# Putting together weight chunks 29 to 40 in SBUF instead of PSUM

## The chip, the core and the metric

One core of a Trainium2 chip runs the whole program once. The metric is the device time of that run in microseconds (us); lower is better. The core has five engines that matter here: PE (TensorE, matrix products), DVE (VectorE) and ACT (ScalarE) for elementwise work, POOL (GpSimd), and SP, which only starts transfers. PSUM is the memory that PE writes its products to, in eight banks; SBUF is the large on-chip memory.

## The reference

Attention with a mask comes first, then two dense blocks on the 1536 tokens that it gives.

```python
x = attention(q, k, v, proj)                  # 2 x 8 heads, 768 tokens, 64 wide -> (1536, 512)
xn = x / sqrt(mean(x * x) + 1e-6) * rms_g
g = xn @ w_gate                               # (512, 1536)
val = xn @ w_val
x = (g * sigmoid(g) * val) @ w_out            # (1536, 512)
h = maximum(x @ w_in, 0)                      # (512, 2048)
out = (h * h) @ w_out2                        # (2048, 512)
```

Inputs and output are float32. PE gets each float32 matrix as a rounded "high" part and the "low" remainder, and computes three products (high by high, high by low, low by high).

## The kernel before

**Weights.** They arrive as 104 chunks of 128 rows by 512 numbers, each as 64-bit floating-point numbers (512 KB). The list `mats` (line 926 on) gives their order: for each of the 12 steps f of the first dense block a gate, a value and an output chunk, all this twice (a first pass for token blocks 0 and 1, a second for 2 and 3), then 32 chunks for the second dense block. A chunk goes through these steps (`plan_weights`):

- SP loads it into `wraw` (3 buffers, line 943).
- ACT takes the absolute value of the upper 32 bits into a work tile (`w_abs`, line 956).
- DVE turns this into a float32 in place with four instructions: line 962 (clamp) and line 967 (two shifts), which read only the work tile, and lines 972 and 976, which join it with the sign and the low bits from `wraw`.
- ACT (line 305), or in some cases POOL (line 309), rounds it to the high part `wih` or `woh`; DVE subtracts for the low part `wil` or `wol` (line 314). Then the work tile is free.

**Where the work tile lies.** `apart(m)` (line 936) decides: inside `mats[WP[0]:WP[1]]` it is a tile `mo`, a PSUM bank; otherwise it is a tile `wv` in SBUF, of which there are four.

```python
t = wst[m]["v"] = mo() if apart(m) else junk()
```

The same `mo` banks take PE's products (lines 1012, 1108, 1119): three banks at first, five after the first half of attention, eight after all of it.

**Dense work around it.** For a step f and a token block PE makes the gate and the value product: 12 instructions of line 1012 each, an "in" block. ACT takes tanh of the gate (1023), DVE multiplies (1027, 1032), ACT or POOL rounds to `yh`, DVE subtracts to `yl`. After every two steps PE makes four output products a token block (1108, an "out" block of 6 instructions) that DVE adds to `acc` (1133). At the end of a pass the sums are split into high and low parts too (`xTF`, `xTG`). The token blocks' inputs are `xTA`, `xTB` in the first pass and `xTD`, `xTE` in the second.

**What sets the order.** A planner (`Plan.run`) walks all instructions with a table of assumed costs, always taking the one that can start first, and so fixes the order of each engine; each engine then runs its list in that order. For a chunk in SBUF the planner assumes 0.335 instead of 0.602 for lines 962 and 967, lets POOL or DVE do the rounding as well as ACT, and keeps DVE and POOL apart in time:

```python
D=0.335 if n < 2 and not far else 0.602, port=not far,
```

Of the kernel before, what the change touches and what calls it, by code (L numbers as in the profile page):

```python
# [54 lines left out]
WR = 3  # L55
WV = 4

WP = (6, 40)
MB = (3, 4)
G = 2  # L60

# [181 lines left out]
def tile_hash_attention_moe(  # L243
# [692 lines left out]
    def apart(m):  # L936

        return m in mats[WP[0]:WP[1]]

# [395 lines left out]
```

## Time and profile before

| what | us |
|---|---|
| median of three runs | 837.7 |
| lowest and highest | 836.83, 839.05 |
| the profiled execution itself | 836.23 |
| its span, first to last instruction | 834.4 |
| PE busy in the span | 793.3 |
| DVE busy in the span | 705.2 |
| ACT busy in the span | 452.4 |
| POOL busy in the span | 223.8 |

A busy time says how long an engine worked, not whether the end waited for it: that is read from the chain that ended last and from the idle time of each engine in a stretch. The start of a row is the time since the first instruction. Matmuls are pipelined: a row of 0.33 us is followed by the next 0.17 us later, so the distance between starts is the price of one.

### The profile page before, as it was taken

What the parts mean: (1) busy time and instruction counts of PE and PEld (TensorE: products, weight loads), DVE (VectorE), ACT (ScalarE), POOL (GpSimd) and SP (SyncE); (2) the same over time, 40 slices, a digit from 0 to 9 for tenths busy, and PEclk for the clock granted to TensorE, in tenths of its full rate; (3) what the DMA queues carried; (4) which work ended last, traced back from release to release, by engine and by line L of the source; (5) the groups of instructions that cost most, each with busy time, mean ns of one, the idle gap of its engine ahead of it and who ended that gap; (6) DMA issues with size and microseconds to landing.
All of it is one profiled execution on the core that took longest, in us unless ns stands there. A gap on an engine that the chain in (4) does not pass through costs nothing.

```text
span 834.4 us, 14958 instructions
## 1 busy us (share of the span) xinstructions
PE 793.3 (95%) x5633; PEld 721.5 (86%) x5633; DVE 705.2 (85%) x1393; ACT 452.4 (54%) x922; POOL 223.8 (27%) x195
## 2 busy tenths in 40 slices
PE   8998887899998998989999999999999999999998
PEld 4787776788887898988889999999899898998996
DVE  6996889798788789989999999999687787877764
ACT  5788887767888677433455344446542242332320
POOL 7578955556567444000000000000000000000000
PEclk8999999999999899999999999999999999999999
DMA  7577784589979797223324334333231120211003
GB/s 224 156 136 145 148 192 127 120 178 177 238 153 187 156 212 171 77 76 101 127 101 148 105 126 129 126 125 95 83 101 45 58 76 30 97 51 51 26 1 151
DMA packets 127728, 100.69 MB, mean 121 GB/s; under 512 B 106548, under 2 KB 108596, under 8 KB 127656
## 3 DMA queue, kind: packets, MB, share of 16 engines
q1 hardware_dynamic: 124160, 90.92, 43.2%
q10 hardware_dynamic: 3496, 8.81, 4.0%
q8 instruction: 44, 0.72, 0.4%
q14 instruction: 28, 0.23, 0.1%
HBM read 67.12 MB, written 3.15 MB: 84 GB/s over the span
## 4 chain that ended last, share of the span: by engine, by line
PE 71%; DVE 20%; ACT 3%; DMA 3%; issue 2%; POOL 1%; ACTq 0%; SPq 0%; DVEq 0%; POOLq 0%
PE mo L1012 33%; PE mo L1119 16%; PE mo L1108 8%; PE S L549 5%; PE O L623 4%; PE S L428 3%; DVE Pa L560 2%; DMA Ta<-hla 2%; DVE mo L962 2%; DVE acc L1133 1%; DVE mo L967 1%; DVE mo L972 1%; DVE Px L560 1%; DVE Tx L314 1%; DVE mo L976 1%
## 5 line engine op out<-in xcount | busy, mean ns | idle before, releaser
L314 POOL TENSOR_TENSOR hla<-Pa,hla 128x768 f16<-128x768 f32 x66 | 110.0, 1669 | 75.1 <-ACT hla L305 67.8
L1133 DVE TENSOR_TENSOR acc<-acc,mo 128x512 f32<-128x512 f32 (+1 forms) x164 | 101.0, 617 | 25.0 <-PE mo L1119 22.9
L549 PE MATMUL S<-k,q 76*128 76x384 f32 (+1 forms) x384 | 92.2, 365 | 12.3 <-DVE Pa L560 7.1
L1038 ACT ACTIVATE mt<-mo 128x384 f32<-128x384 f32 x64 | 31.3, 489 | 100.8 <-PE mo L1012 97.5
L549 PEld LDWEIGHTS S<-k,q 76*128 76x128 f32 (+1 forms) x384 | 65.8, 194 | 18.8 <-DVE Pa L560 9.3
L1119 PE MATMUL mo<-woh,yl 128*128 128x512 f32 x192 | 75.3, 392 | 0.0
L1119 PE MATMUL mo<-wol,yh 128*128 128x512 f32 x192 | 75.2, 392 | 0.0
L1119 PE MATMUL mo<-woh,yh 128*128 128x512 f32 x192 | 74.7, 389 | 0.0
L560 DVE TENSOR_SCALAR_CACHE_REDUCE Pa<-S 128x768 f32<-128x768 f32 x66 | 62.7, 950 | 10.9 <-PE S L549 10.2
L309 POOL TENSOR_SCALAR yh<-mu 128x384 fp32r<-128x384 f32 x20 | 10.8, 541 | 221.6 <-PE mo L1119 88.0
L1042 DVE TENSOR_TENSOR mu<-mt 128x384 f32<-128x384 f32 x64 | 35.4, 553 | 36.0 <-ACT mt L1038 35.9
L1108 PE MATMUL mo<-yh,woh 128*128 128x384 f32 x192 | 64.8, 337 | 0.7 <-ACT woh L305 0.7
L314 DVE TENSOR_TENSOR yl<-mu,yh 128x384 fp32r<-128x384 f32 x112 | 61.8, 559 | 4.1 <-POOL yh L309 2.6
L578 ACT ACTIVATE Pa<-Pa,b 128x768 f32<-128x768 f32 x66 | 62.0, 943 | 5.2 <-DVE sum L631 1.3
L1108 PE MATMUL mo<-yh,wol 128*128 128x384 f32 x192 | 64.5, 336 | 0.1
L1108 PE MATMUL mo<-yl,woh 128*128 128x384 f32 x192 | 64.2, 335 | 0.0
L309 POOL TENSOR_SCALAR wih<-wv 128x512 fp32r<-128x512 f32 x12 | 7.5, 627 | 209.1 <-ACT mt L1038 109.7
L956 ACT ACTIVATE wv<-wraw 128x512 f32<-128x512 f32 x70 | 46.6, 671 | 26.3 <-DMA wraw<-in_w 24.9
L305 ACT CAST hla<-Pa 128x768 f16<-128x768 f32 x66 | 55.0, 835 | 5.8 <-DVE wv L972 1.5
L1012 PE MATMUL mo<-xTAh,wih 128*128 128x384 f32 x160 | 55.2, 345 | 2.3 <-DVE acc L1133 2.3
L1012 PE MATMUL mo<-xTBh,wih 128*128 128x384 f32 x160 | 55.2, 345 | 2.1 <-DVE mu L1032 2.1
L1012 PE MATMUL mo<-xTAh,wil 128*128 128x384 f32 x160 | 54.5, 340 | 0.3 <-DVE wil L314 0.3
(167 smaller groups left out, 2343.8 us busy)
## 6 DMA issues: line engine op xcount, KB each, us to landing
wraw<-in_w SPq DMA_DIRECT2D x104, 512.0 KB
rk<-in_k ACTq DMA_DIRECT2D x14, 384.0 KB
vr<-in_v SPq DMA_DIRECT2D x8, 384.0 KB
out<-acc SPq DMA_DIRECT2D x12, 256.0 KB
q<-q SPq DMA_DIRECT2D x15, 192.0 KB
rq<-in_q ACTq DMA_DIRECT2D x14, 192.0 KB
Ta<-hla SPq DMA_TRANSPOSE x66
rk<-in_k SPq DMA_DIRECT2D x2, 384.0 KB
```

Of the source, the lines that this page charges most:

```text
L305: nc.scalar.copy(out_, in_)
L314: engine[eng].tensor_tensor(out=out_, in0=in0, in1=in1, op=ALU.subtract)
L549: nc.tensor.matmul(sp[:, hf, 0:TB], d[a][0:kr, t * 128:(t + 1) * 128], d[b2][0:kr, hf * TB:(hf + 1) * TB], start=(n == 0), stop=(n == 1),)
L560: nc.vector.tensor_scalar(out=e["P"].rearrange("p (a b) -> p a b", a=2), in0=e["sp"][:, :, 0:TB], scalar1=-1e9 / SCALE, scalar2=None, op0= ...
L578: nc.scalar.activation(e["P"], e["P"], AF.Exp, bias=e["b"], scale=SCALE)
L623: nc.tensor.matmul(d["O"][:, t, 0:w], T[:, a, :], b2[:, c, :], start=(c == 0 and n == 0), stop=(c == QT - 1 and n == 2),)
L956: nc.scalar.activation(t, f32(wst[m]["hi"]), AF.Abs)
L1012: nc.tensor.matmul(ps, a[:, c * 128:(c + 1) * 128], b2[:, c, :], start=(c == 0 and n == 0), stop=(c == 3 and n == 2),)
L1042: nc.vector.tensor_tensor(out=us["u"], in0=st["t"], in1=st["t"], op=ALU.mult)
L1108: nc.tensor.matmul(po, a[:, dc * 128:(dc + 1) * 128], b2, start=(j == 0 and n == 0), stop=(j == len(fs) - 1 and n == 2),)
L1119: nc.tensor.matmul(po, a[:, tt * 128:(tt + 1) * 128], b2, start=(j == 0 and n == 0), stop=(j == len(fs) - 1 and n == 2),)
L1133: nc.vector.tensor_tensor(out=ac, in0=ac, in1=st["p"], op=ALU.add)
```

## The change

One number in the range of chunks that use PSUM.

```diff
-WP = (6, 40)
+WP = (6, 28)
```

The 7th to 28th chunk of `mats` stay in PSUM. The 29th to 40th, twelve chunks, get a `wv` tile in SBUF as all later ones have: the value and output chunks of step 9, all of steps 10 and 11 of the first pass, all of step 0 and the gate of step 1 of the second. Since the planner sees other costs, all engines but SP get another order from there on; the instructions before are the same ones in the same order. PE's list differs over some 412 rows. Its first difference: after the gate of step 9 on `xTA` it now takes the gate on `xTB`, where it took the value on `xTA`.

DVE, where the lists part. First before: `mo` in a weight row is a work tile in PSUM, `wv` one in SBUF.

```order
L962 TENSOR_SCALAR mo<-mo 128x512
L1133 TENSOR_TENSOR acc_2614<-acc_2614,mo 128x384
L967 TENSOR_SCALAR mo<-mo 128x512
L972 SCALAR_TENSOR_TENSOR mo<-wraw,mo 128x512 x2
L1032 SCALAR_TENSOR_TENSOR mu<-mu,mo 128x384
L976 SCALAR_TENSOR_TENSOR mo<-wraw,mo 128x512
L1133 TENSOR_TENSOR acc_2614<-acc_2614,mo 128x384
L962 TENSOR_SCALAR mo<-mo 128x512
L314 TENSOR_TENSOR yl<-mu,yh 128x384 x2
L1133 TENSOR_TENSOR acc_2614<-acc_2614,mo 128x384
```

The same place now, still on DVE.

```order
L962 TENSOR_SCALAR wv<-wv 128x512
L1133 TENSOR_TENSOR acc_2614<-acc_2614,mo 128x384
L967 TENSOR_SCALAR wv<-wv 128x512
L972 SCALAR_TENSOR_TENSOR mo<-wraw,mo 128x512
L972 SCALAR_TENSOR_TENSOR wv<-wraw,wv 128x512
L976 SCALAR_TENSOR_TENSOR mo<-wraw,mo 128x512
L1032 SCALAR_TENSOR_TENSOR mu<-mu,mo 128x384
L1133 TENSOR_TENSOR acc_2614<-acc_2614,mo 128x384
L976 SCALAR_TENSOR_TENSOR wv<-wraw,wv 128x512
L1133 TENSOR_TENSOR acc_2614<-acc_2614,mo 128x384
L314 TENSOR_TENSOR wol<-mo,woh 128x512
L314 TENSOR_TENSOR yl<-mu,yh 128x384 x2
```

The second chunk's clamp (the second line 962) has moved behind the sums into `acc_2614`, and the output chunk (`wol`) is finished earlier.

DVE again, at the end of the first pass, where the last `xTGl` are made. Before:

```order
L314 TENSOR_TENSOR xTGl<-acc_2614,xTGh 128x384 x2
L1027 SCALAR_TENSOR_TENSOR mu<-mt,mo 128x384
L314 TENSOR_TENSOR wil<-wv,wih 128x512
L962 TENSOR_SCALAR wv<-wv 128x512
L972 SCALAR_TENSOR_TENSOR mo<-wraw,mo 128x512
L1027 SCALAR_TENSOR_TENSOR mu<-mt,mo 128x384
L967 TENSOR_SCALAR wv<-wv 128x512
L962 TENSOR_SCALAR wv<-wv 128x512
L972 SCALAR_TENSOR_TENSOR wv<-wraw,wv 128x512
L1032 SCALAR_TENSOR_TENSOR mu<-mu,mo 128x384
```

And now:

```order
L314 TENSOR_TENSOR xTGl<-acc_2614,xTGh 128x384 x2
L1027 SCALAR_TENSOR_TENSOR mu<-mt,mo 128x384
L972 SCALAR_TENSOR_TENSOR wv<-wraw,wv 128x512
L967 TENSOR_SCALAR wv<-wv 128x512
L976 SCALAR_TENSOR_TENSOR wv<-wraw,wv 128x512
L972 SCALAR_TENSOR_TENSOR wv<-wraw,wv 128x512
L1027 SCALAR_TENSOR_TENSOR mu<-mt,mo 128x384
L314 TENSOR_TENSOR wil<-wv,wih 128x512
L976 SCALAR_TENSOR_TENSOR wv<-wraw,wv 128x512
L962 TENSOR_SCALAR wv<-wv 128x512
L967 TENSOR_SCALAR wv<-wv 128x512
L314 TENSOR_TENSOR wil<-wv,wih 128x512
```

The first `wil` here (value of step 1, second pass) stands four weight instructions later behind the `xTGl`; the second (gate of step 2) follows it much sooner.

POOL, from the end of attention on, as a piece of the difference.

```order
-L309 TENSOR_SCALAR yh<-mu 128x384 x4
-L309 TENSOR_SCALAR wih<-wv 128x512 x3
-L309 TENSOR_SCALAR yh<-mu 128x384 x2
+L309 TENSOR_SCALAR yh<-mu 128x384
+L309 TENSOR_SCALAR wih<-wv 128x512
+L309 TENSOR_SCALAR yh<-mu 128x384
+L309 TENSOR_SCALAR xTGh<-acc_2614 128x384
+L309 TENSOR_SCALAR yh<-mu 128x384
+L309 TENSOR_SCALAR woh<-wv 128x512
+L309 TENSOR_SCALAR yh<-mu 128x384
```

POOL takes over the rounding of one weight chunk and of one piece of `xTG` in the changed stretch.

## Rows read from the trace of the kernel before

**Rows 1.** The page's part 4: the chain that ended last, by engine.

```profile
PE 71%; DVE 20%; ACT 3%; DMA 3%; issue 2%; POOL 1%; ACTq 0%; SPq 0%; DVEq 0%; POOLq 0%
```

**Rows 2.** Busy by stretch: PE, PEld, DVE, ACT, POOL, clock, DMA share, GB/s.

```profile
355.00:430.00 75.00, 68.76 (x370) 66.55 (x368) 71.07 (x132) 28.37 (x55) 1.54 (x3) 0.95 0.28 92
...
434.00:596.00 162.00, 161.99 (x923) 160.18 (x922) 157.76 (x315) 74.62 (x141) 9.85 (x16) 1.00 0.38 124
596.00:834.40 238.40, 234.62 (x1178) 212.11 (x1176) 171.30 (x312) 77.72 (x152) 5.59 (x10) 1.00 0.18 60
```

**Rows 3.** PE in time: start, length, instruction, idle before it and its releaser.

```profile
360.39 0.34 PE L1108 MATMUL mo<-yh,wol 128*128 128x384 f32 x1
363.03 0.45 PE L1012 MATMUL mo<-xTAh,wih 128*128 128x384 f32 x1 [2.30 <-DVE acc L1133]
...
376.50 0.41 PE L1108 MATMUL mo<-yh,woh 128*128 128x384 f32 x1 [0.68 <-ACT woh L305]
...
397.40 0.44 PE L1012 MATMUL mo<-xTBh,wih 128*128 128x384 f32 x1 [2.13 <-DVE mu L1032]
...
409.71 0.44 PE L1012 MATMUL mo<-xTDh,wil 128*128 128x384 f32 x1 [0.75 <-DVE wil L314]
...
430.20 0.44 PE L1012 MATMUL mo<-xTDh,wih 128*128 128x384 f32 x1 [0.30 <-ACT wih L305]
431.68 0.44 PE L1012 MATMUL mo<-xTDh,wil 128*128 128x384 f32 x1 [0.86 <-DVE wil L314]
```

**Rows 4.** PE again, two pairs of neighbours after the first long gap.

```profile
365.06 0.53 PE L1012 MATMUL mo<-xTAh,wih 128*128 128x384 f32 x1
365.38 0.53 PE L1012 MATMUL mo<-xTAl,wih 128*128 128x384 f32 x1
...
369.07 0.33 PE L1012 MATMUL mo<-xTBl,wih 128*128 128x384 f32 x1
369.24 0.33 PE L1012 MATMUL mo<-xTBh,wil 128*128 128x384 f32 x1
```

**Rows 5.** Groups of DVE instructions by line, 355 to 432 us: count, busy, mean ns, idle before.

```profile
L967 DVE TENSOR_SCALAR mo<-mo 128x512 uint32<-128x512 uint32 x13 | 9.0, 691 | 0.1
...
L962 DVE TENSOR_SCALAR mo<-mo 128x512 f32<-128x512 f32 x12 | 8.3, 692 | 0.0
L1027 DVE SCALAR_TENSOR_TENSOR mu<-mt,mo 128x384 f32<-128x384 f32 x11 | 6.0, 545 | 3.0 <-ACT mt L1023 3.0
...
L967 DVE TENSOR_SCALAR wv<-wv 128x512 uint32<-128x512 uint32 x3 | 1.3, 418 | 0.0
```

**Rows 6.** DVE in time: neighbours whose starts give the price of each kind.

```profile
356.51 0.69 DVE L962 TENSOR_SCALAR mo<-mo 128x512 f32<-128x512 f32 x1
...
380.32 0.69 DVE L967 TENSOR_SCALAR mo<-mo 128x512 uint32<-128x512 uint32 x1
380.92 0.54 DVE L1133 TENSOR_TENSOR acc<-acc,mo 128x384 f32<-128x384 f32 x1
381.38 0.68 DVE L314 TENSOR_TENSOR wil<-mo,wih 128x512 fp32r<-128x512 f32 x1
...
427.41 0.41 DVE L962 TENSOR_SCALAR wv<-wv 128x512 f32<-128x512 f32 x1
427.75 0.68 DVE L972 SCALAR_TENSOR_TENSOR wv<-wraw,wv 128x512 uint32<-128x512 uint32 x1
...
430.95 0.68 DVE L314 TENSOR_TENSOR wil<-wv,wih 128x512 fp32r<-128x512 f32 x1
```

**Rows 7.** POOL and DVE in time, where a POOL copy overlaps a DVE instruction.

```profile
420.70 0.51 POOL L309 TENSOR_SCALAR yh<-mu 128x384 fp32r<-128x384 f32 x1 [28.45 <-PE mo L1108]
...
420.83 0.93 DVE L976 SCALAR_TENSOR_TENSOR wv<-wraw,wv 128x512 uint32<-128x512 uint32 x1
```

**Rows 8.** DVE in time: its two longest idle pieces between 434 and 500 us.

```profile
444.84 0.43 DVE L962 TENSOR_SCALAR wv<-wv 128x512 f32<-128x512 f32 x1 [0.72 <-ACT wv L956]
467.58 0.56 DVE L1027 SCALAR_TENSOR_TENSOR mu<-mt,mo 128x384 f32<-128x384 f32 x1 [1.44 <-ACT mt L1023]
```

## The prediction

> **What bounds the kernel now.** I read the chain that ended last first: PE has 71% of it, DVE 20% [rows 1]. A mean over stages hides where the 20% lie, so the busy times by stretch come next [rows 2]. From 434 to 596 us PE works 161.99 of 162 us, and from 596 to the end 234.62 of 238.4, where what is missing is the last store. There PE is the bound, and whatever starts it earlier ends the program earlier. From 355 to 430 us it works 68.76 of 75 us while DVE works 71.07 and the mean clock is 0.95: there DVE is the bound. This is the stretch of the twelve chunks. So the third view is PE in time [rows 3]: the reader should see six of PE's seven waits (the seventh is 0.2), each for a product of DVE or for an ACT step that stands right behind one: a sum that frees a bank (2.30), a high part of an output weight (0.68), a `mu` (2.13), low parts of weights (0.75 and 0.86), a high part (0.30). The fourth view shows what the long gaps cost afterwards [rows 4]: 1.2 us after the gap of 2.30 neighbouring matmuls start 0.32 us apart instead of 0.17, the lower of the two clock levels (1.2 instead of 2.4 GHz), for some eleven instructions; eleven times 0.147 is 1.6 us.
>
> **How much PE can win at most.** From the last matmul before the first gap (start 360.39, next slot 360.56) to the matmul that starts at 431.68 [rows 3] PE makes 20 in-blocks of 12 and 16 out-blocks of 6 instructions, then two more. At 0.1733 us each (0.17 between neighbours at the higher clock [rows 4]) that is 20 x 2.08 + 16 x 1.04 + 0.35 = 58.6 us. It takes 71.1 us. So 12.5 us are gaps and low clock, more than the 7 us of idle time that the rows print, because a row's modelled end covers some of each gap. 12.5 us is the ceiling.
>
> **What the change takes from DVE.** Twelve chunks, two instructions each (lines 962 and 967), go from PSUM to SBUF. In this same stretch they last 692 and 691 ns on `mo`, 418 on `wv` [rows 5]; what DVE pays is the distance between starts: 0.60 on `mo` (380.32 to 380.92), 0.34 on `wv` (427.41 to 427.75) [rows 6]. The saving is 24 x 0.26 = 6.2 us. Lines 972 and 976 and the subtract also change memory, but they last the same on `mo` and on `wv` (the `mo` and `wv` subtracts both 0.68 [rows 6]); nothing there. ACT's steps have both forms too and ACT is busy 28.4 of 75 us [rows 2], so a few hundredths for each are hidden; were they not, 24 of them at 0.04 would be 1 us. SP's list is the same, and a load's buffer is freed by line 976, which comes earlier.
>
> **How this reaches PE.** I follow the DVE list from 356.51, where the lists part, to the low part of the second pass's step-2 gate, for which PE waits until 431.68 [rows 3, 6]. Before, 132 instructions lead there: 68 weight steps at 0.60, 59 of 384 columns at 0.465 (0.46 between 380.92 and 381.38), 5 fast ones at 0.34; in all 69.9 us. The real way is 430.95 + 0.60 - 356.51 = 75.0. The 5.1 us between are DVE's own waits, 3.0 of them for tanh [rows 5], and small dependences. In the new list 126 instructions lead there: 42 at 0.60, 56 at 0.465, 28 at 0.34, in all 60.8 us, 9.1 less. 6.0 of this are 23 faster instructions, the rest six others now put behind it (three at 0.60, three at 0.465: 3.2). If all waits stay, this low part is ready at 431.55 - 9.1 = 422.4; gapless, PE would ask for it at 431.68 - 12.5 = 419.2. The 3.0 us of waits for tanh should go: they stand at a place where PE had just lost 2.3 us to a bank and 1.6 to the clock, and two more free banks remove that first wait. (That PE has no bank is what the releaser of 363.03 says: a sum, line 1133, frees one. The two work tiles of the step-9 value and the step-10 gate held two of eight there.)
>
> In return DVE, now faster, reaches sums before PE has finished them. Placing both lists side by side at these prices, the first five weights are in time by 0.5 to 3 us, and the step-1 value of the second pass is late: PE would ask at 414.7, and DVE has it at 415.3 without any wait, near 416.8 with 1.5 us of waits. Its four weight steps now stand behind all of `xTG`. So PE stops there for about 2 us. The six instructions that were put behind must then be done before the next output blocks: 3.2 us, of which I leave half on the path, 1.5. That half also stands for a low clock after the 2 us gap (1.6 by rows 4, if it comes). Sum: 12.5 - 2.0 - 1.5 = **9.0 us**. Against the profiled execution (836.2, span 834.4) that gives 827.2; the median lies 1.5 above that execution, so **828.7**.
>
> **A price that only appears in SBUF.** At 420.83 line 976 on a `wv` lasts 0.93 instead of 0.68 us, while POOL copies from 420.70 to 421.21 [rows 7]: 0.25 lost. In the changed stretch POOL makes some six copies; DVE's list now offers more that they can hit. Six at 0.25 to 0.35 are 1.5 to 2.1 us at worst, and nothing if each falls beside an instruction that reads PSUM, or while PE is ahead. I take nothing beyond the reserve above and keep 2.1 for the range.
>
> The Trainium skill (SBUF — State Buffer, Who interferes with whom) speaks against the change here: a DVE instruction that uses both SBUF port pairs, or reads two SBUF inputs while GpSimd reads, blocks fully until the other is done. Its price for one copy is then the copy's whole length, an estimate of 0.5 to 0.6, and the gain would be 9.0 - 6 x 0.55 = 5.7 us. The row agrees in direction but shows half the price.
>
> **The rivals.**
>
> *Only DVE's own saving arrives.* If DVE meets as many waits as now (for sums, tanh, high parts of ACT), it ends the stretch 6.2 us earlier, not 9. For it: the sums of a block of four cannot be taken faster than PE makes them, 1.04 us apart. Against it: 3.0 of the waits have a cause that goes. 837.7 - 6.2 = 831.5; with the port's 2.1, 833.6.
>
> *The gain is given back after 434 us.* DVE works 157.76 of 162 us there [rows 2]; its largest pauses are 0.72 and 1.44 [rows 8]. If PE gets ahead by 2 us more than DVE, it may run dry there. Each dry spell like those of now costs 2.3 and 1.5 for the clock; two give 837.7 - 9 + 7.6 = 836.3, no change. Against it: DVE is early by about as much as PE (9.1 and 9), the order there is nearly the same, and DVE was on time from the same kind of start (PE waiting for it at 431.68).
>
> *Slower: the four `wv` tiles.* A chunk's first ACT step must wait until the subtract of the fourth chunk before it is done, and ACT, in order, keeps tanh and casts waiting behind it; PE then has no bank and no weight. With PSUM there were eight. If this holds PE by 1.3 us a chunk, 12 x 1.3 = 15.6 eat the 12.5: 837.7 - 12.5 + 15.6 = 840.8; it decides from 1.04 us a chunk on. Against it: from 434 us on all chunks go through these four tiles at the same pace, and PE has no gap [rows 2].
>
> That the change does not do what it says is hardly possible: the same two lines show both prices within this stretch [rows 5].
>
> **How the numbers follow.** The forecast (8 to 12.5 us won) gets 0.60, only DVE's saving (4 to 8 won) 0.22, given back 0.10, slower 0.06; 0.02 is left for more than the ceiling. Faster or slower by over 0.3% is 2.5 us, about what a measurement of this kernel can tell from no change. Faster: 0.60 + 0.22 + 0.02 = 0.84; same 0.10; slower 0.06. The range takes in the first two cases with the port's price: 837.7 - 12.5 = 825.2 to 833.6.
>
> **What would show it right or wrong.** Lines 962 and 967 run twelve times less on `mo` and twelve times more on `wv`, there at about 0.42 us. The gap of 2.30 at 360.7 and the low clock behind it are gone. PE's idle time up to its last wait falls from 7 to about 2 us, its largest piece at a low part of a weight some 14 us before PE becomes gapless. From there to the end the trace is the old one, earlier. I am wrong if PE has new gaps after 425 us (rival two), if ACT waits for a subtract before line 956 (rival three), or if the lines on `wv` last clearly longer than 0.42 on average (the port).

## The result, and the profile after

| | before | after |
|---|---|---|
| median of five runs, us | 837.7 | 832.02 |
| lowest and highest, us | 836.14, 839.82 | 827.13, 832.87 |
| profiled execution, us | 836.23 | 829.23 |
| its span, us | 834.4 | 827.4 |
| PE, DVE busy, us | 793.3, 705.2 | 790.9, 697.8 |

The ratio is 0.9914, with a 95% interval of 0.9889 to 0.9938: by the ratio 7.2 us are won, by the medians 5.7. The same kernel timed again, beside 23 runs of before, gave 0.9928 (0.9911 to 0.9944), 6.0 us. The forecast was 9.0.

First the chain that ended last, by engine, of the kernel after.

```profile
PE 58%; DVE 30%; DMA 4%; issue 3%; ACT 2%; POOL 1%; ACTq 0%; SPq 0%; DVEq 0%; POOLq 0%
```

DVE's share is larger than before (20% [rows 1]), though DVE works 7.4 us less and the kernel is shorter. The chain names one releaser at each step; where PE and DVE keep pace, either may be named. The share says where to look and isn't a price.

Busy time by stretch (PE, PEld, DVE, ACT, POOL, clock, DMA share, GB/s). The stretches are times since the first instruction, so from 425 us on each holds work that came up to 8 us later before:

```profile
355.00:425.00 70.00, 67.82 (x377) 66.48 (x376) 67.91 (x138) 29.70 (x55) 3.86 (x5) 0.98 0.36 113
...
434.00:596.00 162.00, 161.16 (x909) 158.16 (x908) 149.95 (x301) 74.38 (x140) 8.05 (x13) 1.00 0.36 117
596.00:827.40 231.40, 227.66 (x1144) 206.00 (x1142) 170.14 (x310) 74.44 (x147) 5.55 (x10) 1.00 0.19 62
```

Against [rows 2]: PE lacked 6.2 us of work in the 75 of the old first stretch and lacks 2.2 of 70 now; the stretch from 434 to 596, all but gapless before, now lacks 0.8. From the first instruction of line 1119 on nothing differs but where it starts: the rest takes 251.0 us before (834.4 less 583.4) and 250.9 now (827.4 less 576.5).

PE in time (start, length, instruction, idle before and its releaser): the place of the old gap of 2.30, the first of the instructions that waited, and the old last wait.

```profile
360.00 0.33 PE L1012 MATMUL mo<-xTAh,wih 128*128 128x384 f32 x1
...
414.64 0.34 PE L1012 MATMUL mo<-xTEh,wil 128*128 128x384 f32 x1
416.65 0.44 PE L1012 MATMUL mo<-xTDh,wih 128*128 128x384 f32 x1 [1.67 <-ACT wih L305]
...
417.67 0.44 PE L1012 MATMUL mo<-xTDh,wil 128*128 128x384 f32 x1 [0.40 <-DVE wil L314]
...
419.12 0.52 PE L1012 MATMUL mo<-xTDh,wih 128*128 128x384 f32 x1
419.44 0.52 PE L1012 MATMUL mo<-xTDl,wih 128*128 128x384 f32 x1
...
422.31 0.34 PE L1012 MATMUL mo<-xTEl,wih 128*128 128x384 f32 x1
...
423.55 0.33 PE L1012 MATMUL mo<-xTDh,wil 128*128 128x384 f32 x1
...
548.88 0.34 PE L1108 MATMUL mo<-yl,woh 128*128 128x384 f32 x1
550.04 0.44 PE L1108 MATMUL mo<-yh,wol 128*128 128x384 f32 x1 [0.82 <-DVE wol L314]
```

The bank gap at the start (2.30 [rows 3]) is gone, and of the seven waits of before none is left at its place. Three are new: two for the step-1 value weight of the second pass (1.67 and 0.40), with a low clock behind them (neighbours 0.32 apart; the granted clock from 419.1 to 422.3 us is 0.50, the level of 1.2 GHz), and some 132 us later 0.82 for an output weight. The step-2 gate's third instruction starts at 423.55 instead of 431.68 [rows 3], 8.1 us earlier.

DVE's lines from 355 to 425 us (count, busy, mean ns, idle before):

```profile
L962 DVE TENSOR_SCALAR wv<-wv 128x512 f32<-128x512 f32 x15 | 6.5, 436 | 0.3 <-ACT wv L956 0.3
L967 DVE TENSOR_SCALAR wv<-wv 128x512 uint32<-128x512 uint32 x15 | 6.2, 418 | 0.1
...
L1027 DVE SCALAR_TENSOR_TENSOR mu<-mt,mo 128x384 f32<-128x384 f32 x11 | 6.0, 545 | 0.0
```

The two lines now run on `wv` at 436 and 418 ns instead of 692 and 691 on `mo`, and the 3.0 us for which line 1027 waited for tanh [rows 5] are 0.0.

### The profile page after: what moved, and what is told of

The parts are those of the page before. It is cut to its first block, busy times and chain, and to the rows that moved or that the text cites. A ratio compares the mean times of both kernels' runs of the same rounds, so it can differ in the third digit from the quotient of the medians.

```text
span 827.4 us, 14953 instructions
## 1 busy us (share of the span) xinstructions
PE 790.9 (96%) x5633; PEld 720.2 (87%) x5633; DVE 697.8 (84%) x1393; ACT 454.1 (55%) x923; POOL 224.2 (27%) x194
## 4 chain that ended last, share of the span: by engine, by line
PE 58%; DVE 30%; DMA 4%; issue 3%; ACT 2%; POOL 1%; ACTq 0%; SPq 0%; DVEq 0%; POOLq 0%
PE mo L1012 23%; PE mo L1119 16%; PE S L549 5%; PE O L623 5%; PE mo L1108 4%; DMA wraw<-in_w 3%; DVE acc L1133 3%; PE S L428 3%; DVE wv L976 2%; DVE wv L972 2%; DVE Pa L560 2%; DVE mu L1027 2%; DVE wv L962 2%; DVE wil L314 2%; DVE mu L1032 1%
## 5 line engine op out<-in xcount | busy, mean ns | idle before, releaser
L956 ACT ACTIVATE wv<-wraw 128x512 f32<-128x512 f32 x82 | 54.3, 671 | 33.6 <-DMA wraw<-in_w 32.9
L976 DVE SCALAR_TENSOR_TENSOR wv<-wraw,wv 128x512 uint32<-128x512 uint32 x82 | 57.5, 703 | 0.2
L972 DVE SCALAR_TENSOR_TENSOR wv<-wraw,wv 128x512 uint32<-128x512 uint32 x82 | 56.3, 690 | 0.2
L309 POOL TENSOR_SCALAR wih<-wv 128x512 fp32r<-128x512 f32 x9 | 5.7, 637 | 185.2 <-ACT mt L1038 109.7
L305 ACT CAST wih<-wv 128x512 fp32r<-128x512 f32 x40 | 24.9, 622 | 55.7 <-DVE wv L976 55.4
```

Source lines behind the costliest of these rows:

```text
L305: nc.scalar.copy(out_, in_)
L956: nc.scalar.activation(t, f32(wst[m]["hi"]), AF.Abs)
L972: nc.vector.scalar_tensor_tensor(out=t, in0=hi, scalar=0xC0000000, in1=t, op0=ALU.bitwise_and, op1=ALU.bitwise_or)
L976: nc.vector.scalar_tensor_tensor(out=t, in0=lo, scalar=29, in1=t, op0=ALU.logical_shift_right, op1=ALU.bitwise_or)
```

## Where the expected gain went

Counted as in the prediction, from the instruction that waited 2.30 before (360.00 now), PE takes 63.55 us up to 423.55 for the same 338 instructions, which need 58.6. So 4.95 of the ceiling of 12.5 are left: 1.84 from the slot after 414.64 (414.81) to 416.65; 0.67 more up to 417.67, two instructions for 1.02 us; 1.69 for the low clock and its edges (17 instructions from 417.67 to 422.31 take 4.64 instead of 2.95); and 0.75 in small pieces before. Then 1.0 is lost at 550.04, whose slot was 549.05, and 0.1 in the instruction itself.

Why the weight is late shows in DVE and ACT just before:

```profile
414.32 0.68 DVE L972 SCALAR_TENSOR_TENSOR wv<-wraw,wv 128x512 uint32<-128x512 uint32 x1
414.93 0.42 DVE L967 TENSOR_SCALAR wv<-wv 128x512 uint32<-128x512 uint32 x1
415.26 0.68 DVE L976 SCALAR_TENSOR_TENSOR wv<-wraw,wv 128x512 uint32<-128x512 uint32 x1
...
416.93 0.68 DVE L314 TENSOR_TENSOR wil<-wv,wih 128x512 fp32r<-128x512 f32 x1
...
418.93 0.69 DVE L314 TENSOR_TENSOR wil<-wv,wih 128x512 fp32r<-128x512 f32 x1
```

```profile
415.98 0.62 ACT L305 CAST wih<-wv 128x512 fp32r<-128x512 f32 x1 [0.47 <-DVE wv L976]
```

DVE works without a pause. PE could have started this weight's product at 414.81, but its last DVE step ends only at 415.94, since it stands behind the `xTGl` in DVE's list; ACT rounds it by 416.60, and DVE has the low part at 417.61. The place is the one that the prediction named. The last row is the low part of the step-2 gate: DVE has it done at 419.6, four microseconds before PE takes it at 423.55. So DVE's total is not what is late here; one weight is, by its place in DVE's list.

And at 550 us, the output weight's low part, of after and then of before:

```profile
549.31 0.68 DVE L314 TENSOR_TENSOR wol<-wv,woh 128x512 fp32r<-128x512 f32 x1
```

```profile
556.55 0.68 DVE L314 TENSOR_TENSOR wol<-wv,woh 128x512 fp32r<-128x512 f32 x1
```

PE took this weight, in the kernel before, at the second of these rows:

```profile
556.93 0.34 PE L1108 MATMUL mo<-yl,woh 128*128 128x384 f32 x1
557.28 0.45 PE L1108 MATMUL mo<-yh,wol 128*128 128x384 f32 x1
```

The place was tight already: 0.35 us lie between the two instead of 0.17, since the low part ended at 557.23. Now DVE is 7.2 us earlier there and PE came 8.1 earlier, so PE waits. At this place PE can win no more than DVE has won up to it.

## The experiments

Theory A: DVE's time is what the stretch up to 434 us lacks, and what is won follows DVE's instruction times. Rival B: the two freed banks do it. Rival C: the planner's new order does it. The measure beside the total is the time from the first `xTDl` (line 318) to the first matrix weight of the second dense block (line 1119): before 248.4 us (335.0 to 583.4), after 242.1 (334.4 to 576.5). It leaves out attention, which varies from run to run.

**The changed kernel again**, without an edit.

> The changed kernel itself, timed beside the others. Forecast 5 to 9 us below the kernel before. If the wait for the low part of the step-1 value weight (second pass) and the low clock behind it come back, the profile again shows one gap of 1.5 to 2.5 us on PE near 416 us and no gap before it.

Measured: median 832.37, ratio 0.9928 (0.9911 to 0.9944); the stage took 240.8 us (339.1 to 579.9), 7.6 less than before.

```profile
421.30 0.44 PE L1012 MATMUL mo<-xTDh,wih 128*128 128x384 f32 x1 [1.75 <-ACT wih L305]
...
424.16 0.33 PE L1012 MATMUL mo<-xTEh,wih 128*128 128x384 f32 x1
424.33 0.33 PE L1012 MATMUL mo<-xTEl,wih 128*128 128x384 f32 x1
```

The same wait at the same instruction, 0.08 longer, yet the neighbours behind it stay 0.17 apart: no low clock followed this time. The wait belongs to the kernel; the low clock behind it comes in one execution and not in another.

**The old order, twelve chunks in SBUF.** Planner and all lists stay those of before, and only the memory of the twelve chunks changes, with a fifth `wv` tile because the old order holds them longer. Both banks are freed, DVE's two lines are fast, the order is old.

```diff
-        return pers.tile([128, 512], F32, tag="wv", name="wv", bufs=WV)
+        return pers.tile([128, 512], F32, tag="wv", name="wv", bufs=WV + 1)
...
-        t = wst[m]["v"] = mo() if apart(m) else junk()
+        t = wst[m]["v"] = mo() if apart(m) and m not in mats[28:40] else junk()
```

> The twelve chunks lie in SBUF, but every engine keeps the order of the kernel before (the planner is told nothing; the work tiles in SBUF are five). Theory A (DVE's 6.2 us are what counts): 5 to 7 us below before, about as good as the change. Theory B (the freed banks count): also below before, by some 3 to 5 us. Theory C (the new order makes the gain): no more than 2 us below before.

Measured: median 830.4, ratio 0.9909 (0.9889 to 0.9929); stage 241.6 us (334.7 to 576.3), 6.8 less. PE's two longest waits between 355 and 440 us:

```profile
401.90 0.44 PE L1012 MATMUL mo<-xTDh,wih 128*128 128x384 f32 x1 [1.13 <-ACT wih L305]
...
424.36 0.44 PE L1012 MATMUL mo<-xTDh,wil 128*128 128x384 f32 x1 [0.86 <-DVE wil L314]
```

The gain is whole without the new order, so C falls as its source. The order only decides for which weight PE waits.

**The old order, SBUF, but DVE slow.** The same, with the lines 962 and 967 of these chunks written as two-input instructions, whose second input is one number a partition, spread over the columns. They compute the same values. The banks are freed; DVE's time isn't.

```diff
+            if n == 0:
+                nc.vector.scalar_tensor_tensor(
+                    out=t, in0=t, scalar=TINY, in1=where["huge"].to_broadcast([128, 512]), op0=ALU.max, op1=ALU.min
+                )
```

> As the run before, but lines 962 and 967 of the twelve chunks are written as instructions with two tensor inputs, which should again cost DVE 0.60 us each: SBUF and free banks, no faster DVE. Theory A: the time of the kernel before within 2 us. Theory B: keeps 3 to 5 us of the gain, since the 2.3 us gap at 360 us was for a bank and takes 1.6 us of low clock with it. The profile tells by that gap.

Measured: median 839.71, ratio 1.0013 (0.9993 to 1.0033); stage 249.0 us (336.8 to 585.8). In this kernel line 963 is the clamp, 968 the shifts, 1024 stands for 1012 and 1120 for 1108. DVE's lines, then PE in time:

```profile
L963 DVE SCALAR_TENSOR_TENSOR wv<-wv,huge 128x512 f32<-128x512 f32 x12 | 8.4, 698 | 0.0
L968 DVE SCALAR_TENSOR_TENSOR wv<-wv,mask 128x512 uint32<-128x512 uint32 x12 | 8.2, 683 | 0.0
...
L1039 DVE SCALAR_TENSOR_TENSOR mu<-mt,mo 128x384 f32<-128x384 f32 x11 | 6.0, 547 | 0.8 <-ACT mt L1035 0.8
```

```profile
362.86 0.33 PE L1024 MATMUL mo<-xTAh,wih 128*128 128x384 f32 x1
...
407.89 0.44 PE L1024 MATMUL mo<-xTDh,wih 128*128 128x384 f32 x1 [2.18 <-ACT wih L305]
...
409.37 0.69 PE L1024 MATMUL mo<-xTDh,wil 128*128 128x384 f32 x1 [0.86 <-DVE wil L314]
...
410.18 0.52 PE L1024 MATMUL mo<-xTDl,wih 128*128 128x384 f32 x1
410.50 0.52 PE L1024 MATMUL mo<-xTDh,wil 128*128 128x384 f32 x1
...
433.69 0.45 PE L1024 MATMUL mo<-xTDh,wil 128*128 128x384 f32 x1 [0.86 <-DVE wil L314]
```

This is the run that decides against B. The bank gap is gone (362.86 starts without a wait, where before PE waited 2.30 [rows 3]), and line 1027's (here 1039's) wait for tanh is 0.8 instead of 3.0. Yet nothing is won: PE waits for weights instead, 2.18 and 0.86 at 408 to 409 us, and the last wait of 0.86 stands as before. By their edits, only DVE's speed lies between this run and the one above: 7.4 us of the stage, 9.3 of the median. Some of it is not DVE's time itself. Behind the wait of 2.18 sixteen neighbours start 0.32 apart, which is 16 x 0.147 = 2.4 us, and the run above has no such stretch. Outside the stage this profile is 2.8 us longer too, 2.1 of it in attention.

**The new order, DVE slow.** The changed kernel with the same two-input instructions.

> The changed kernel with its order, the chunks in SBUF, but lines 962 and 967 of the twelve chunks at 0.60 us as in the run before. Theory A: 5 to 7 us slower than the changed kernel, so the time before within 2 us. Theory B: 1 to 3 us slower than the changed kernel. Theory C: the changed kernel's time.

Measured: median 838.0, ratio 0.9995 (0.9979 to 1.0011); stage 247.2 us (338.0 to 585.2). One line of DVE and PE's longest wait there:

```profile
L963 DVE SCALAR_TENSOR_TENSOR wv<-wv,huge 128x512 f32<-128x512 f32 x12 | 8.5, 706 | 0.0
```

```profile
426.05 0.45 PE L1024 MATMUL mo<-xTDh,wih 128*128 128x384 f32 x1 [2.01 <-ACT wih L305]
```

New order, SBUF, free banks, and no gain. This gives the cleanest price of DVE's time: neither this profile nor the second one of the changed kernel has a low clock in the stage, and their difference is 6.4 us (247.2 less 240.8), beside 24 x 0.26 = 6.2. So the four kernels give one answer: with DVE fast 0.9909 and 0.9914 to 0.9928, with DVE slow 1.0013 and 0.9995, whichever the order. A stands.

**Six chunks instead of twelve.**

```diff
-WP = (6, 28)
+WP = (6, 34)
```

> Half the dose: only the last six of the twelve chunks (35th to 40th) go to SBUF. If DVE's time in the bound stretch is what counts, 6 x 2 x 0.26 = 3.1 us are won, half of the change's 6: about 835. If one single wait made the gain (the bank at 360 us, before these chunks), nearly nothing is won; if a wait behind 386 us made it, all 6.

Measured: median 835.57 beside 838.99, ratio 0.996 (0.9942 to 0.9978); stage 245.3 us (337.9 to 583.2), 3.1 less.

```profile
366.44 0.44 PE L1012 MATMUL mo<-xTAh,wih 128*128 128x384 f32 x1 [2.79 <-DVE acc L1133]
```

Half the chunks, half the gain, with the bank gap still there and even longer than the 2.30 of before. A gain that came from the bank would have been missing here.

**Eighteen chunks.**

```diff
-WP = (6, 28)
+WP = (6, 22)
```

> A larger dose: six more chunks (23rd to 28th), put together while attention ends, go to SBUF too. If DVE's time counts there as well, up to 3.1 us less than the changed kernel; POOL still subtracts for attention until some 330 us, so by the port theory two or three of the six lose what they gain, and the result is the changed kernel's time within 2 us.

Measured: median 829.64, ratio 0.9884 (0.9858 to 0.9909), some 3 us better than with twelve. (The order changes ahead of the first `xTDl` here, so the stage can't be compared.) PE still waits 1.66 at the value weight of step 1, with a low clock behind it.

**The late weight, first cure.** The splitting of the first pass's sums (`xTF`, `xTG`) gets a later rank in the planner, so that DVE takes the weight's steps ahead of it: the last `xTGl` now stands some 115 instructions later in DVE's list.

```diff
             tag, p = xt_place[2, blk]
             xb = ("xT", 2, blk)
             fresh = xb not in plan.bufs
+            rank += 60 * (blk < 2)
```

> The changed kernel, with the eight high and low parts of the second block's inputs (xTF, xTG), which nothing reads before 560 us, given a later rank in the planner. If DVE's work in the bound stretch is the bound, 8 x 0.465 = 3.7 us leave it, the gap near 416 us and its low clock go, and 2 to 5 us more are won (827 to 830). If PE is held by something else there, or DVE has no room later, the time stays within 1.5 us of the changed kernel.

Measured: median 826.92, ratio 0.9852 (0.9824 to 0.9881); stage 238.8 us (335.0 to 573.8), 9.6 less than before. Busy by stretch as above, then PE in time: a place in the second pass's step 1 where a block on `xTE` follows one on `xTD`, and the one long wait that is left:

```profile
355.00:425.00 70.00, 69.75 (x399) 68.71 (x398) 68.41 (x139) 31.71 (x59) 3.59 (x6) 1.00 0.38 120
```

```profile
415.65 0.33 PE L1012 MATMUL mo<-xTDh,wil 128*128 128x384 f32 x1
415.82 0.33 PE L1012 MATMUL mo<-xTEh,wih 128*128 128x384 f32 x1
...
546.97 0.44 PE L1108 MATMUL mo<-yh,wol 128*128 128x384 f32 x1 [0.83 <-DVE wol L314]
```

The waits at the value weight and the low clock behind them are gone, and PE lacks 0.25 of 70 us instead of 2.18. Together they had cost 3.3 us of the stage in the execution with the low clock (242.1 less 238.8) and 2.0 in the one without (240.8). The wait for `wol` at 547 us stays.

**The late weight, second cure.** This weight alone (the 41st chunk) gets an earlier rank.

```diff
-                    plan_weights(m, rank + R_W)
+                    plan_weights(m, rank + R_W - 4 * (m == mats[40]))
```

> The changed kernel, with the step-1 value chunk of the second pass (the one PE waits for near 416 us) ranked earlier in the planner; on DVE it changes only who comes first after the xTG low parts: its last steps come before two multiplications. If that one weight is all that PE lacks, the gap shrinks by the 0.5 to 1 us that it gets earlier; if DVE's total up to there is the bound, the wait appears again at the next product and the time is the changed kernel's within 1 us.

Measured: median 832.11, ratio 0.9928 (0.9902 to 0.9955); stage 240.5 us (336.3 to 576.8): no gain over the changed kernel. The profile has the wait still, shorter and without a low clock behind it, and new ones follow: 0.38 for an output weight at 428 us, 0.67 for the next gate and 0.28 for its low part:

```profile
417.93 0.44 PE L1012 MATMUL mo<-xTDh,wih 128*128 128x384 f32 x1 [1.24 <-ACT wih L305]
...
432.60 0.44 PE L1012 MATMUL mo<-xTDh,wih 128*128 128x384 f32 x1 [0.67 <-ACT wih L305]
```

In DVE's list the weight's last steps moved ahead of two instructions of line 1027, still behind the last `xTGl`; and the next gate's weight is late instead.

**Both edits that paid**: the later splitting and eighteen chunks.

> The changed kernel with both edits that paid alone: the copies of the transposed rows of the second pass put behind (the run with that edit alone had no gap of PE near 416 us and took 826.9 us, ratio 0.985) and the chunks from the 23rd on put together in SBUF instead of from the 29th on (alone 829.6 us, ratio 0.988, about 3 us below the changed kernel's 0.9914 to 0.9928). If DVE's time in the stretch up to 434 us is still what PE waits for, the two add up: 826.9 - 3 = about 824, ratio near 0.981. If the second pass has become PE's own with the first edit, the further 6 chunks save DVE time that nothing waits for: 826 to 828, ratio 0.984 to 0.987.

Measured: median 822.56 beside 839.33, ratio 0.9817 (0.979 to 0.9843), the best of all kernels here. Busy by stretch:

```profile
355.00:425.00 70.00, 69.80 (x407) 69.48 (x406) 69.69 (x144) 35.85 (x67) 2.71 (x3) 1.00 0.38 121
...
434.00:596.00 162.00, 162.00 (x912) 159.03 (x912) 151.33 (x306) 75.57 (x141) 11.16 (x14) 1.00 0.36 114
```

The two gains add up. PE works through from 355 to 596 us but for 0.2; even the wait for `wol` at 547 is gone, as DVE is earlier still.

**The later splitting and 24 chunks** (the range 6 to 16).

> As the run beside it, with the chunks from the 17th on in SBUF (12 more than the changed kernel). The further chunks fall before the place where PE ran out of work, in the first pass of the step and the end of the part before it. If DVE's time anywhere there counts, a further gain of 1 to 3 us over the run beside it: 821 to 823. If PE is the bound by then, the same as the run beside it within 1 us. If chunks that are put together in SBUF during the attention part take DVE or POOL time that this part needs, slower than the run beside it by 1 to 4 us.

Measured: median 827.41, ratio 0.9864 (0.984 to 0.9888), 4.9 us slower than the run beside it. PE's longest waits between 300 and 400 us:

```profile
331.15 0.44 PE L1012 MATMUL mo<-xTAh,wih 128*128 128x384 f32 x1 [1.52 <-ACT wih L305]
...
345.47 0.44 PE L1108 MATMUL mo<-yh,woh 128*128 128x384 f32 x1 [0.75 <-POOL woh L309]
...
354.73 0.44 PE L1012 MATMUL mo<-xTAh,wil 128*128 128x384 f32 x1 [0.84 <-DVE wil L314]
```

The six more chunks begin between 249 and 303 us, during attention, and weights that follow come late, from ACT, POOL and DVE. The clock from 100 to 200 us was lower in this execution than in the run beside it (0.90, 0.95), but that isn't where the time went: at 340 us both have started 540 instructions of lines 1012 and 1108. At 360 us it is 608 here and 629 there, so 21 x 0.1736 = 3.6 us are lost in these 20 us. Most of the rest is lost near 548 us, where the wait for `wol` is back (0.83). Why these weights are late wasn't taken apart.

## Why the prediction was right in its sign and too large in its size

**The bound stretch and the price: right.** DVE bounds the stretch, its two lines cost 0.26 less each, and the new prices are those of the rows (436 and 418 ns).

**The vanishing waits: right for DVE, wrong as a gain of PE's.** The bank gap and the 3.0 us of tanh waits went as said, and DVE itself came out as forecast: the low part of the step-2 gate starts at 418.93 instead of 430.95, 12.0 us earlier, and 9.1 + 3.0 were expected. PE came only 8.1 us earlier, because it had stopped at an earlier weight. And the runs with a slow DVE show that both waits can go and nothing is won. In the old order tanh waits fell from 3.0 to 0.8, yet DVE's idle time from 355 to 432 us stayed (3.6 and 3.75): it now waited for PE's products (1.5) and for ACT's first step (0.8). Take such a wait away, and the lateness turns up at the next product.

**The late weight: right place, 0.5 too small.** Forecast 2.0 for the step-1 value; it took 1.84 + 0.67 = 2.5. I looked for the largest wait at the low part; it came at the high part, ACT's step ahead of it, which waits for the same DVE step.

**The term that failed is the last one**, 1.5 for the "half" of 3.2 that it left on the path, which "also stands for a low clock". One number stood for two costs that both came. The low clock alone took 1.69. The other came later than expected: 1.1 at 550 us, at a place where I expected the old trace, just earlier. That the six instructions put behind are what came due there is argued, not shown. With 0.75 of small pieces that makes 3.5 instead of 1.5. So 2.5 + 3.5 = 6.0 stayed on the path instead of 3.5, and 12.5 - 6.0 = 6.5 were won; the stage shows 6.3 (248.4 less 242.1). In the second execution of the changed kernel the low clock did not come, and the stage shows 7.6: then 4.9 stayed. One reading was off besides: the slow neighbours of the kernel before begin 1.4 us after the gap, not 1.2, and are ten, not eleven, 1.5 us instead of 1.6.

**The range held, the central case did not.** 8 to 12.5 us won had a chance of 0.60; by the medians and the ratios 5.7 to 7.2 were won, the first rival's 4 to 8, which had 0.22. The time lies in the range because the range took in both.

**The rivals.** The size is that of the first rival, 6.2, though not by its reason: DVE met far fewer waits than before (63.1 us from 356.45 to the end of that low part for 60.8 of work, so 2.3 instead of 5.1), and PE lost the difference at one weight and in the clock. The run with the later splitting takes that loss away, and the stage gives 9.6. The second rival came in a small piece, 1.1 us. The third did not: ACT's first step on a chunk waits for loads (9.1 of its 9.2 us of idle time), as ACT's line from 355 to 425 us shows:

```profile
L956 ACT ACTIVATE wv<-wraw 128x512 f32<-128x512 f32 x16 | 10.5, 672 | 9.2 <-DMA wraw<-in_w 9.1
```

**The port.** Five POOL copies in the stretch, not six, and they met two DVE instructions (POOL, then DVE):

```profile
383.90 0.62 POOL L309 TENSOR_SCALAR wih<-wv 128x512 fp32r<-128x512 f32 x1 [23.27 <-DVE wv L976]
```

```profile
384.10 0.70 DVE L962 TENSOR_SCALAR wv<-wv 128x512 f32<-128x512 f32 x1
```

0.70 instead of 0.42 is 0.28 lost; the other, line 976 at 360.31, lost 0.17 (0.85 instead of 0.68). That is 0.45 of the 1.5 to 2.1 kept for the range. The trace shows more than these two. From 355 to 560 us thirteen instructions of lines 962, 967, 972 and 976 on `wv` start at least 0.07 us after a POOL copy that still runs, and each ends 0.27 or 0.28 us (962, 967) or 0.53 or 0.54 us (972, 976) after that copy's end. The Trainium skill (SBUF — State Buffer, Who interferes with whom) says that the second of two such instructions is blocked until the first is done, and the trace agrees. What it doesn't bear out is the price that the prediction took from this, the copy's whole length: the loss is what is left of the copy less some 0.14 us (0.42 left and 0.28 lost, 0.32 left and 0.17 lost). That the estimate of 5.7 us is near the result is chance, since only two such meetings came in the stretch and they cost 0.45.

## What to carry to other kernels

Where one engine bounds a stretch, cost a change by that engine's own time first. Waits elsewhere that "will go" are its shadow: add them to the sum only if a reason says that they don't come back at the next product. When a planner reorders for a faster step, look for the product that it now makes last, and give each cost left on the path its own term; taking the work ahead of that one product away was worth 2.0 to 3.3 us of the stage, beside the 6.3 to 7.6 of the change.

## What the runs showed of the hardware that was not expected

**The same wait, with and without a low clock behind it.** After 1.67 us of waiting PE ran at the lower level for ten instructions in one execution of the changed kernel; after 1.75 us in another execution it did not, and neither did it after 1.13 in the old order with SBUF nor after 2.01 in the new order with slow DVE, 1.24 in the second cure and 1.52 with 24 chunks. After 1.66 (eighteen chunks), 2.13 and 2.30 (both before), 2.18 (old order, slow DVE) and 2.79 (six chunks) it did. So the 1.5 us or so behind a gap is a cost that may come, and not a fixed part of the gap.

**Attention and the clock vary together.** The two profiles of the changed kernel differ by 3.5 us of span (827.4, 830.9), although the dense stage was 1.3 shorter in the longer one. The stretch from 100 to 200 us of the one and of the other (clock in the third column from the end):

```profile
100.00:200.00 100.00, 88.53 (x922) 78.10 (x923) 88.29 (x184) 77.93 (x172) 58.66 (x47) 0.95 0.71 161
```

```profile
100.00:200.00 100.00, 89.43 (x912) 78.57 (x911) 86.78 (x179) 77.48 (x167) 57.10 (x45) 0.91 0.72 159
```

Of the nine profiles whose edits touch only what comes behind the first `xTDl`, the six with a clock of 0.95 there reach it at 334.4 to 336.8 us, the two with 0.93 at 337.9 and 338.0, and the one with 0.91 at 339.1. Which of the two makes the other isn't shown. The difference between totals is therefore less sharp than the difference between stages.

**Memory isn't the only thing that sets DVE's time.** The clamp and the shifts take 418 to 436 ns in SBUF with constants, but 698 and 683 ns in the same SBUF tile with a second input of one number a partition: as long as on PSUM (692, 691). The Trainium skill (VectorE: DVE Perf Modes, Why `tensor_tensor` can't do 2×_2P or 4×) gives a reason, for `tensor_tensor`: the fast form fetches two elements of one tensor over both read ports, and a second tensor takes one of the two. These rows, of another instruction with two inputs, agree with it.
